# A state-space and feed-forward mix: the first strip moved ahead of tile 1's turns, and the second product cut at 384 columns instead of 512

## The chip, the cores and the metric

The kernel runs on one core of one Trainium2 chip. Times are device microseconds (us) of one execution of the program. A profile is one such execution, recorded instruction by instruction; its span, from the program's first instruction to its last, is about 1.8 us shorter than the time on the clock of the same run. A *run* below is one timed execution, and a *ratio* is the mean time of one kernel's fast runs over that of the other's of the same rounds, so it is not quite the ratio of the medians that are quoted.

Engines in the profile: PE is TensorE, PEld its weight loads, DVE is VectorE, ACT is ScalarE, POOL is GpSimd, SP issues most DMAs. "L268" is line 268 of that kernel. Lines shift by one to three between the two kernels.

## The reference

```python
x = A_x                                            # (1, 2048, 640) bf16
g = sigmoid((x * gate_w).sum(-1, keepdims=True))
# a: diagonal complex state space: Bu = x @ B_bar, h_t = Lam_bar * h_{t-1} + Bu_t, a = 2 Re(C h) + x * Dskip
# b: b = gelu(x @ w1 + b1) @ w2 + b2               # 640 -> 1728 -> 640
return g * a + (1 - g) * b
```

The sequence is taken in four chunks of 512 positions; a tile is 128 positions. Two parts matter here. The *first product* is x @ w1 for chunk 0, at the start of the program, while its data are still arriving. The *second product* is gelu(...) @ w2, once for each chunk.

## The kernel before

The start. TensorE needs x with the feature dimension on partitions. For chunk 0 it makes that itself: a *turn* is a product with the identity, whose result VectorE or ScalarE copies from PSUM to SBUF. A *strip* is six products of 128 columns, one for each of six PSUM banks: one tile's contribution of one block of 128 features. The warm-up products (ones times ones) use TensorE before any data is there.

```python
pA = bank()
for n in (512, 512, 512, 512, 512, 512, 128, 128):          # warm-up
    nc.tensor.matmul(pA[:, 0:n], lhsT=ones(P), rhs=ones(n), start=True, stop=True)
...
def turn_first(a, other):
    t = bank()
    turn(t, 0, a, 0)                                        # feature block 0 -> t, VectorE copies
    turned(nc.vector, t, 0, a, 0, 1)
    turn(other, a * P, a, 1)                                # feature block 1 -> other, ScalarE copies
    turned(nc.scalar, other, a * P, a, 1, 2)

turn_first(0, pA)
turn_first(1, bank())
...
banks = [bank() for _ in range(FA)]                         # FA = 6; the pool has 8 banks
...
part(0, 0)              # part(kd, a): the strip of feature block kd on tile a
part(0, 1)
turn_first(2, pA)
part(1, 0)
part(1, 1)
turn_first(3, pA)
part(0, 2)
turn_rest(0, bank(), (nc.scalar, KA, KD))                   # feature blocks 2 to 4 of tile 0
part(1, 2)
...
```

The second product. The 640 output columns of a tile are cut in a wide piece and a rest; each piece is 13 products (and one pair of half-row products). Two tiles' rests share a bank.

```python
MAIN, REST = (0, 512), (512, D)                             # D = 640
def biased(c, kind, i):                                     # ScalarE writes the bias into a fresh bank
    ...
    nc.scalar.activation(out=v, in_=src, func=ACT.Identity)
def fin_b(c, at={}):
    ...
    for h in range(2):
        for j in range(H):
            full(opened[c, "wide", a], 0, a, *MAIN)         # 13 products of 512 columns
            ...
        for j in range(H):
            full(opened[c, "rest", h], j * P, h * H + j, *REST)   # 13 products of 128 columns
        if h == 0:
            half_rows()
```

Of the kernel before, what the change touches and what calls it, by code (L numbers as in the profile page):

```python
# [16 lines left out]
P = 128  # L17
T = 2048
D = 640
# [9 lines left out]
H = TPC // 2  # L29
# [12 lines left out]
def kernel(  # L42
# [19 lines left out]
    nc = tc.nc  # L62
# [12 lines left out]
    def bank(dtype=F32):  # L75
        return ps.tile([P, CH * 4 // (4 if dtype == F32 else 2)], dtype, name="bank")
# [113 lines left out]
    class Clock:  # L190
        pe = 3.4
        act = 12.0
# [8 lines left out]
    def let_out(until, chunk=-1):  # L201
        while pend:
            ready, cost, fn, _ = pend[0]
            start = max(ck.dve, ready)
            if start >= until and not any(x[3] == chunk for x in pend if chunk >= 0):
                return
            pend.pop(0)
            fn()
            ck.dve = start + cost
# [6 lines left out]
    def pe(cols):  # L216
        ck.pe += cols / 2400.0 + 0.002

    def act(cost):
        ck.act = max(ck.act, ck.pe + 0.2) + cost  # L220
        return ck.act
# [4 lines left out]
    nc.vector.tensor_copy(out=tf[:], in_=tfi[:])  # L226
    ones = lambda n: nc.const_aps.tensor(1.0, [P, n], BF16)
    pA = bank()
    for n in (512, 512, 512, 512, 512, 512, 128, 128):
        nc.tensor.matmul(pA[:, 0:n], lhsT=ones(P), rhs=ones(n), start=True, stop=True)  # L230

    def turn(p, col, a, kd):
        nc.tensor.matmul(p[:, col:col + P], lhsT=xn[0][:, a, kd * P:(kd + 1) * P], rhs=ident[:], start=True, stop=True,  # L233
                         skip_group_check=True)

    def turned(engine, p, col, a, k0, k1):
        dst = xT[0][:, k0:k1, a * P:(a + 1) * P]
        src = p[:, col:col + (k1 - k0) * P].rearrange("p (k t) -> p k t", t=P)
        if engine is nc.vector:
            nc.vector.tensor_copy(out=dst, in_=src)  # L240
        else:
            nc.scalar.activation(out=dst, in_=src, func=ACT.Identity)  # L242

    def turn_first(a, other):
        t = bank()
        turn(t, 0, a, 0)
        turned(nc.vector, t, 0, a, 0, 1)
        turn(other, a * P, a, 1)
        turned(nc.scalar, other, a * P, a, 1, 2)

    turn_first(0, pA)
    turn_first(1, bank())

    def col(name, dtype=F32, n=KS):
        return const.tile([P, n], dtype, name=name)
# [68 lines left out]
    banks = [bank() for _ in range(FA)]  # L324

    def strip(kd, t0, t1, first, f0=0, f1=FA):
        for kf in range(f0, f1):
            ff1_mm(banks[kf], 0, kf, kd, t0, t1, first, 3)
# [30 lines left out]
    def part(kd, a):  # L359
        strip(kd, a * P, (a + 1) * P, kd == 0)  # L360

    part(0, 0)
    part(0, 1)
    turn_first(2, pA)
    part(1, 0)
    part(1, 1)
    turn_first(3, pA)
    part(0, 2)
# [217 lines left out]
            dve_now(ck.pe, 0.45, lambda: nc.vector.tensor_tensor(out=p[:, 0:d1 - d0], in0=xn[c][:, a, d0:d1], in1=Dbc[:, d0:d1], op=ALU.mult))  # L586
            seeded[ti].append(p)

    MAIN, REST = (0, 512), (512, D)
    opened = {}  # L590

    def biased(c, kind, i):
        p = bank()
        d0, d1 = MAIN if kind == "wide" else REST
        n = 1 if kind == "wide" else H
        v, src = p[:, 0:n * (d1 - d0)], b2bc[:, d0:d1]
        if n > 1:
            v = v.rearrange("p (j d) -> p j d", j=n)
            src = src.rearrange("p (o d) -> p o d", o=1).to_broadcast([P, n, d1 - d0])
        nc.scalar.activation(out=v, in_=src, func=ACT.Identity)  # L600
        act(0.6 if n == 1 else 0.4)
        opened[c, kind, i] = p

    def first_banks(c):
        biased(c, "wide", 0)
        biased(c, "wide", 1)

    def fin_b(c, at={}):
        def full(p, col, a, d0, d1):
            for kf in range(KF - 1):  # L610
                nc.tensor.matmul(p[:, col:col + d1 - d0], lhsT=gel[c][:, kf, a * P:(a + 1) * P], rhs=w2_sb[:, kf, d0:d1],  # L611
                                 start=False, stop=False, skip_group_check=True)
                pe(d1 - d0)

        def out_of(p, col, a, d0, d1):
            ti = c * TPC + a
            if gbs[ti] is None:
                gbs[ti] = fwork.tile([P, D], F32, name="gb")
            nc.scalar.activation(out=gbs[ti][:, d0:d1], in_=p[:, col:col + d1 - d0], func=ACT.Identity, scale=gcol[:, 1, ti:ti + 1])  # L619
            act(0.7 if d1 - d0 > 320 else 0.4)  # L620

        def half_rows():
            for d0, d1 in (MAIN, REST):
                for j in range(H):
                    for h in range(2):
                        p, col = (opened[c, "wide", h * H + j], 0) if d0 == 0 else (opened[c, "rest", h], j * P)
                        nc.tensor.matmul(p[:, col:col + d1 - d0], lhsT=gelL[c % 2][h * F_LAST:(h + 1) * F_LAST, j, :],  # L627
                                         rhs=w2l[h * F_LAST:(h + 1) * F_LAST, d0:d1], start=False, stop=True, skip_group_check=True)
                    pe(d1 - d0)
            ck.pe += 0.2  # L630

        biased(c, "rest", 0)
        biased(c, "wide", 2)
        for h in range(2):
            for j in range(H):
                a = h * H + j
                full(opened[c, "wide", a], 0, a, *MAIN)
                if a == 0:
                    biased(c, "wide", 3)
                    biased(c, "rest", 1)  # L640
                if h == 1:
                    out_of(opened[c, "wide", a], 0, a, *MAIN)
                if a in at:
                    at[a]()
                let_out(ck.pe)
            for j in range(H):
                full(opened[c, "rest", h], j * P, h * H + j, *REST)
            if h == 0:
                half_rows()
                for j in range(H):  # L650
                    out_of(opened[c, "wide", j], 0, j, *MAIN)
            for j in range(H):
                out_of(opened[c, "rest", h], j * P, h * H + j, *REST)
            let_out(ck.pe)

    def fin_a(c, at={}):
# [36 lines left out]
    ssm(1, {KS - 1: lambda: first_banks(0)})  # L693
    gates(1)
    fin_b(0, {a: (lambda a=a: fold(a)) for a in range(3)})
    gel_tile(2)
    ff1(2, 0, {1: lambda: fold(3), 4: lambda: fold(4), 9: lambda: seed(0), 11: lambda: seed(1)})
    gates(2)
    fin_a(0)
    load_xn(2)  # L700
    ssm(2, {KS - 1: lambda: first_banks(1)})
    fin_b(1, seeds(1))
    fin_a(1)
    load_xn(3)
    ssm(3)
    gel_tile(3)
    ff1(3, 0, {KF - 3: lambda: first_banks(2)})
    fin_b(2, seeds(2))
    gates(3)
    fin_a(2, {TPC - 1: lambda: first_banks(3)})  # L710
# [33 lines left out]
```

## Time and profile before

| | before |
|---|---|
| median, range of the 3 runs at hand | 216.24 us, 216.13 to 216.39 |
| profiled run: time, span | 215.6 us, 213.8 us |
| PE busy | 98% of the span |
| first product with the second block of w1's columns (w1b) starts | 12.45 us |
| last product starts | 210.87 us |

The profiled run is not one of the three timed ones, and it was 0.5 us shorter than the shortest of them.

The page's busy times and its chain of waits (the chain of work that ended last, as shares of the span):

```profile
PE 208.6 (98%) x1384; PEld 117.0 (55%) x1403; DVE 189.1 (88%) x389; ACT 103.4 (48%) x188; POOL 1.0 (0%) x13
...
PE 96%; DMA 1%; issue 1%; SPq 0%; DVE 0%; ACT 0%
```

TensorE is the chain almost throughout; the 1% of DMA is one load at the start. The timeline of PE shows it (columns: start, length of the group, engine, line, operation, form, how many, and in brackets the idle time before it and what ended that):

```profile
0.77 2.93 PE L230 MATMUL bank<-const-bfloat16-1.0 128*128 128x512 bf16 x8 [0.77 <-PEq L728]
3.50 0.42 PE L233 MATMUL bank<-ident,xn 128*128 128x128 bf16 x2
4.30 0.29 PE L233 MATMUL bank<-ident,xn 128*128 128x128 bf16 x2 [0.39 <-DMA xn<-in_A_x_dram]
4.42 1.08 PE L268 MATMUL bank<-xT,w1a 128*128 128x128 bf16 x12
5.34 0.28 PE L233 MATMUL bank<-ident,xn 128*128 128x128 bf16 x2
5.45 0.83 PE L268 MATMUL bank<-xT,w1a 128*128 128x128 bf16 x12
6.12 0.28 PE L233 MATMUL bank<-ident,xn 128*128 128x128 bf16 x2
6.23 0.50 PE L268 MATMUL bank<-xT,w1a 128*128 128x128 bf16 x6
6.72 0.33 PE L233 MATMUL bank<-ident,xn 128*128 128x128 bf16 x3
```

Read it in steps. The turns of tile 0 are the row at 3.50. Tile 1's turns wait until 4.30 for their load. The next twelve products take 1.08 us and the twelve after them 0.83: the first group stands still for 0.25 us after its fifth product, until a bank is free. Tile 3's turns (6.12) come after tile 2's (5.34); the turns at 6.72 come after tile 3's, and wait for tile 3's copy.

A group's length hides a second thing. The warm-up's products of 512 columns start 427 ns apart and those of 128 columns 107 ns apart; from 4.30 us on, 128 columns take 55.8 ns. The TensorE clock is halved at first. The trace's own clock record says "full" from 4.10 us on. The summary rows of granted clock do not show it: they give 1.0 from the start, because the record begins only with the first change.

### The profile page before, as it was taken

The page shows a single profiled execution, that of the slowest core. Times are in us where ns is not written, and L with a number is a line of the kernel's source. Part 1 is how long each engine was busy: PE and PEld are TensorE (multiplying, and loading weights), DVE is VectorE, ACT ScalarE, POOL GpSimd, SP SyncE. Part 2 cuts the span into 40 slices and gives each one's busy share as a digit, 9 for nine tenths or more (in the row PEclk, how much of TensorE's full clock was granted, in tenths as well). Part 3 has the DMA queues.
Part 4 walks back from the last instruction along what each step waited for, and adds up shares of the span by engine and source line. Part 5 has one row for each costly group of instructions (what it writes and reads, how often), then busy time and mean ns, then how long its engine had stood idle before and what let it go on. Part 6 is the DMA issues. An engine that isn't in the chain of part 4 may idle for free.

```text
span 213.8 us, 3572 instructions
## 1 busy us (share of the span) xinstructions
PE 208.6 (98%) x1384; PEld 117.0 (55%) x1403; DVE 189.1 (88%) x389; ACT 103.4 (48%) x188; POOL 1.0 (0%) x13
## 2 busy tenths in 40 slices
PE   7999999999999999999999999999999999999994
PEld 3845444454454544775445577444455577664773
DVE  1599999999999999999999999999999999983153
ACT  3699956675839688203563210455683422204200
POOL 1000000000000000000000000000000000000000
PEclk9999999999999999999999999999999999999999
DMA  6869999997000000051000006100000000100011
GB/s 192 243 157 191 205 186 290 313 210 185 0 0 0 3 0 0 14 183 65 0 0 3 0 0 186 62 0 2 3 0 14 0 3 31 61 34 0 0 66 61
DMA packets 31572, 15.84 MB, mean 74 GB/s; under 512 B 22979, under 2 KB 31555, under 8 KB 31555
## 3 DMA queue, kind: packets, MB, share of 16 engines
q1 hardware_dynamic: 30850, 14.99, 28.9%
q10 hardware_dynamic: 704, 0.62, 1.0%
q8 instruction: 11, 0.18, 0.4%
q14 instruction: 7, 0.05, 0.1%
HBM read 7.48 MB, written 2.62 MB: 47 GB/s over the span
## 4 chain that ended last, share of the span: by engine, by line
PE 96%; DMA 1%; issue 1%; SPq 0%; DVE 0%; ACT 0%
PE bank L611 26%; PE bank L268 26%; PE bank L670 20%; PE bank L553 20%; DMA xn<-in_A_x_dram 1%; PE bank L627 1%; PE bank L294 1%; PE bank L233 1%; SPq L136 0%; DVE ot L675 0%; ACT xT L242 0%; PE bank L284 0%; PE bank L402 0%; PE bank L371 0%
## 5 line engine op out<-in xcount | busy, mean ns | idle before, releaser
L611 PE MATMUL bank<-w_sb,gel 128*128 128x128 bf16 (+1 forms) x408 | 57.1, 298 | 0.6 <-issue 0.3
L611 PEld LDWEIGHTS <-gel 128*128 128x128 bf16 x416 | 32.2, 98 | 25.6
L556 ACT ACTIVATE bu<-bank 128x512 bf16<-128x512 f32 x40 | 23.7, 606 | 37.3 <-PE bank L553 37.3
L273 ACT ACTIVATE gel<-bank,colB 128x512 bf16<-128x512 f32 x52 | 33.7, 695 | 11.1 <-PE bank L268 10.4
L670 PEld LDWEIGHTS <-hs 128*128 128x128 bf16 x330 | 31.5, 98 | 11.6
L507 DVE TENSOR_TENSOR_SCAN g<-r_c,carry,v 128x512 bf16<-128x512 f32 x30 | 37.3, 1269 | 0.0
L619 ACT ACTIVATE gb<-bank,gcol 128x512 f32<-128x512 f32 (+1 forms) x32 | 15.1, 526 | 32.7 <-PE bank L627 17.8
L268 PE MATMUL bank<-xT,w1a 128*128 128x512 bf16 (+1 forms) x170 | 27.6, 311 | 0.3
L670 PE MATMUL bank<-CT_im,hs 128*128 128x320 bf16 (+2 forms) x165 | 27.1, 295 | 0.0
L670 PE MATMUL bank<-CT_re,hs 128*128 128x320 bf16 (+2 forms) x165 | 27.1, 295 | 0.0
L675 DVE SCALAR_TENSOR_TENSOR ot<-bank,gcol,gb 128x320 bf16<-128x320 f32 (+2 forms) x33 | 17.4, 532 | 8.9 <-PE bank L670 8.7
L553 PE MATMUL bank<-xT,BT_im 128*128 128x512 bf16 x99 | 24.8, 379 | 0.1
L553 PE MATMUL bank<-xT,BT_re 128*128 128x512 bf16 x97 | 24.5, 379 | 0.2
L268 PEld LDWEIGHTS <-w1a 128*128 128x128 bf16 x174 | 14.1, 98 | 11.7 <-issue 0.2
L268 PE MATMUL bank<-xT,w1b 128*128 128x512 bf16 x80 | 17.9, 379 | 0.0
L586 DVE TENSOR_TENSOR bank<-xn,Dbc 128x320 f32<-128x320 bf16 (+2 forms) x33 | 14.4, 480 | 3.7 <-ACT gb L619 3.6
L553 PEld LDWEIGHTS <-BT_im 128*128 128x128 bf16 x100 | 9.8, 98 | 11.8
L488 DVE TENSOR_TENSOR v<-wa,wb 128x512 bf16<-128x512 bf16 x40 | 15.2, 420 | 0.6
L553 PEld LDWEIGHTS <-BT_re 128*128 128x128 bf16 x100 | 9.6, 98 | 11.0
L600 ACT ACTIVATE bank<-b2bc 128x512 f32<-128x512 bf16 (+1 forms) x24 | 11.7, 526 | 6.7 <-DVE ot L675 6.7
L488 DVE TENSOR_TENSOR wa<-TCOS,g 128x1024 bf16<-128x1024 bf16 x20 | 13.7, 685 | 0.1
L268 PE MATMUL bank<-xT,w1c 128*128 128x512 bf16 x57 | 13.6, 379 | 0.2
(101 smaller groups left out, 166.4 us busy)
## 6 DMA issues: line engine op xcount, KB each, us to landing
out_dram<-ot SPq DMA_DIRECT2D x15, 160.0 KB, 1.8
w_sb<-in_B_w_dram SPq DMA_DIRECT2D x1, 2080.0 KB
xn<-in_A_x_dram SPq DMA_DIRECT2D x3, 640.0 KB
w1b<-in_B_w_dram SPq DMA_DIRECT2D x5, 128.0 KB, 3.7
w1c<-in_B_w_dram SPq DMA_DIRECT2D x5, 112.0 KB, 4.4
w1a<-in_B_w_dram ACTq DMA_DIRECT2D x2, 192.0 KB, 3.3
w1a<-in_B_w_dram SPq DMA_DIRECT2D x1, 384.0 KB, 3.7
xn<-in_A_x_dram SPq DMA_DIRECT2D x4, 64.0 KB, 3.3
```

The costliest lines, as they stand in the source:

```text
L268: nc.tensor.matmul(p[:, t0:t1], lhsT=w, rhs=xT[c][:, kd, t0:t1], start=(kd == 0) if first is None else first, stop=(kd == last), skip_grou ...
L273: nc.scalar.activation(out=gel[c][:, kf, :], in_=p[:, :], func=ACT.Gelu_apprx_tanh, bias=b1_c[:, kf:kf + 1])
L488: nc.vector.tensor_tensor(out=o, in0=a, in1=b, op=op)
L507: nc.vector.tensor_tensor_scan(s["g"][:, ri, :], r_c[:, ks:ks + 1].to_broadcast([P, CH]), s["v"][:, ri, :], init, ALU.mult, ALU.add)
L553: nc.tensor.matmul(p[:], lhsT=BT[ks >= KSA][:, kd, (ks % KSA if ks < KSA else ks - KSA) * P:][:, 0:P], rhs=xT[c][:, kd, :], start=(kd == 0 ...
L556: nc.scalar.activation(out=bu[:, ri, :], in_=p[:], func=ACT.Identity)
L586: dve_now(ck.pe, 0.45, lambda: nc.vector.tensor_tensor(out=p[:, 0:d1 - d0], in0=xn[c][:, a, d0:d1], in1=Dbc[:, d0:d1], op=ALU.mult))
L600: nc.scalar.activation(out=v, in_=src, func=ACT.Identity)
L611: nc.tensor.matmul(p[:, col:col + d1 - d0], lhsT=gel[c][:, kf, a * P:(a + 1) * P], rhs=w2_sb[:, kf, d0:d1], start=False, stop=False, skip_ ...
L619: nc.scalar.activation(out=gbs[ti][:, d0:d1], in_=p[:, col:col + d1 - d0], func=ACT.Identity, scale=gcol[:, 1, ti:ti + 1])
L670: nc.tensor.matmul(p[:, 0:d1 - d0], lhsT=hs[c][:, j, lo:lo + P], rhs=CT[:, j % KS, d0:d1], start=False, stop=(j == 2 * KS - 1), skip_group ...
L675: nc.vector.scalar_tensor_tensor(out=ot[:, d0:d1], in0=p[:, 0:d1 - d0], scalar=gcol[:, 0, ti:ti + 1], in1=gbs[ti][:, d0:d1], op0=ALU.mult, ...
```

## The change

Part A fills the wait for tile 1's load with the first strip, uses one bank fewer, shortens the warm-up, and puts three filler products under tile 0's copy. Part B cuts the second product at 384 columns, so that the pieces are more even (384 and 256 in place of 512 and 128).

```diff
-    for n in (512, 512, 512, 512, 512, 512, 128, 128):
+    for n in (512, 512, 512, 512, 512, 128, 128, 128, 128):
...
     turn_first(0, pA)
-    turn_first(1, bank())
...
+    for _ in range(3):
+        nc.tensor.matmul(banks[0][:, 0:P], lhsT=ones(P), rhs=ones(P), start=True, stop=True, skip_group_check=True)
     part(0, 0)
+    turn_first(1, pA)
+    part(1, 0)
     part(0, 1)
     turn_first(2, pA)
-    part(1, 0)
     part(1, 1)
     turn_first(3, pA)
...
-    MAIN, REST = (0, 512), (512, D)
+    WIDE = 3 * P
+    MAIN, REST = (0, WIDE), (WIDE, D)
```

The rest of the diff adapts column offsets (`j * P` to `j * (D - WIDE)`) and the cost figures by which the program, while it is built, orders VectorE's and ScalarE's work.

More of the change, by code (lines that the diff above doesn't have):

```diff
@@ L600, in biased @@
         nc.scalar.activation(out=v, in_=src, func=ACT.Identity)
-        act(0.6 if n == 1 else 0.4)
+        act(0.5 if n == 1 else 0.6)
         opened[c, kind, i] = p
@@ L619, in out_of @@
             nc.scalar.activation(out=gbs[ti][:, d0:d1], in_=p[:, col:col + d1 - d0], func=ACT.Identity, scale=gcol[:, 1, ti:ti + 1])
-            act(0.7 if d1 - d0 > 320 else 0.4)
+            act(0.56 if d1 - d0 > 320 else 0.45)
         def half_rows():
@@ L625, in half_rows @@
                     for h in range(2):
-                        p, col = (opened[c, "wide", h * H + j], 0) if d0 == 0 else (opened[c, "rest", h], j * P)
+                        p, col = (opened[c, "wide", h * H + j], 0) if d0 == 0 else (opened[c, "rest", h], j * (D - WIDE))
                         nc.tensor.matmul(p[:, col:col + d1 - d0], lhsT=gelL[c % 2][h * F_LAST:(h + 1) * F_LAST, j, :],
@@ L646, in fin_b @@
             for j in range(H):
-                full(opened[c, "rest", h], j * P, h * H + j, *REST)
+                full(opened[c, "rest", h], j * (D - WIDE), h * H + j, *REST)
             if h == 0:
@@ L652, in fin_b @@
             for j in range(H):
-                out_of(opened[c, "rest", h], j * P, h * H + j, *REST)
+                out_of(opened[c, "rest", h], j * (D - WIDE), h * H + j, *REST)
             let_out(ck.pe)
```

## The prediction

> **What bounds the kernel.** TensorE. The page gives PE 98% of the 213.8 us span, the chain of waits 96% on PE; the table of waits shows PE idle 1.5 us, nearly all before 4.3 us. DVE is 88% busy but PE does not wait for it after 7 us. Only PE time can move the result.
>
> **Part A, the start.** In the timeline of before: warm-up products from 0.77 us, one per 427 ns (512 columns) or 107 ns (128) at the low clock; turns of tile 0 at 3.50; idle until tile 1's load lands at 4.25; five strip products, then 0.25 us standing until ScalarE's copy (ends 4.90) frees a bank; then nearly gapless, 55.8 ns per 128-column product; tile 3's turns at 6.12.
> The change makes the warm-up 0.21 us shorter (first turn about 3.29), adds three fillers (0.3 us under the first copy, free), and puts strip 0 of tile 0 into the wait for tile 1's load. One bank fewer is taken, so the 0.25 us bank wait goes. Reckoned from those durations: strip 3.98 to 4.37, tile 1's turns, next strip 4.56 (second weight block lands 4.51), strip 0 of tile 1 at 4.98 (behind its copy), tile 2's turns 5.31, next strip until 5.76, where before stood at 6.12: 0.36 us ahead. But tile 3's load landed at 5.91, so its turns go at about 5.96 instead of 6.12: about 0.16 us survives. After it the order is as before, with the same copy waits, and later loads have slack.
>
> **Part B, 384 + 256 columns for 512 + 128.** Product and column counts stay (13 x 16 pairs plus half rows). Measured start to start: 215.5 ns at 512 columns, 55.8 at 128, 82.5 at 192: columns/2.4 plus about 2.4 ns, which agrees with the Trainium skill, "TensorE: Matmul & The Clock Gate", section "Back-to-back issue gap". A pair costs 271.3 ns before and, by that estimate, 271.5 after. The same section also states about 81 ns per product for a stream with weight loads at N=128; then the 128-column pieces would waste 25 ns x 208 = 5 us and this part would pay. The trace contradicts it: 26 in a row at 55.8 ns, each 98 ns weight load hidden. The switch into and out of the half rows costs 96 and 93 ns, by the drain, whatever the width. So part B is worth 0. ScalarE moves the same columns in as many instructions; VectorE's seeds come slightly earlier. Neither is on the chain.
>
> **Total.** 216.24 - 0.2 = **216.05 us**, range 215.7 to 216.35. Faster by over 2%: 0.01; within 2%: 0.98; slower by over 2%: 0.01.
>
> **What would show it.** A right: first strip near 4.0 us, no PE wait for tile 1's load, a short new wait for tile 3's load near 5.9, every later stage earlier by one constant 0.1 to 0.4 us. B right: stages of the second product last as long as before, PE idle unchanged, products spaced near 162 and 109 ns.
>
> **What would make it wrong.** The clock reached full at 4.10 us; if that comes later, strips run at 107 ns and the lead vanishes. If tile 3's load lands earlier, the gain nears 0.4 us. If narrow pieces cost something that the trace hides, B gains. If banks are freed later because 256-column pieces finish in pairs, PE waits at the next stage's start.

## More of the kernel before

ScalarE opens the banks with the bias and takes the results out.

In the last chunk, two such openings are placed just before the opening of the bank of the first product's last tile:

```python
ff1(3, 0, {KF - 3: lambda: first_banks(2)})     # first_banks: biased(c, "wide", 0), biased(c, "wide", 1)
# inside ff1, at the same step: last = last_bank(c)   (ScalarE opens it with b1x; TensorE waits for that)
```

## The result and the profile after

| | before | changed |
|---|---|---|
| median of 6 runs, range | 216.09 us, 215.83 to 216.39 | 215.68 us, 215.48 to 215.95 |
| ratio | | 0.998, 95% interval 0.9968 to 0.9993 |
| span of the profiled run | 213.8 us | 214.0 us |
| first w1b product | 12.45 us | 12.73 us |
| last product | 210.87 us | 211.06 us |
| clock record: full from | 4.10 us | 5.50 us |

The six runs of before include the three from which the prediction was made. The measured median lies 0.02 us below the predicted range. And the two profiles contradict the medians: the profiled run of the changed kernel is 0.2 us *longer* than that of before.

The page after, the same lines:

```profile
PE 210.5 (98%) x1407; PEld 126.5 (59%) x1407; DVE 189.4 (88%) x389; ACT 103.3 (48%) x188; POOL 1.0 (0%) x13
...
PE 98%; DVE 0%; issue 0%
```

The DMA share has left the chain, as intended. (The product counts are not comparable: by its weight loads the program has 1403 products before and 1407 after, one warm-up product and three fillers more, and 19 records are missing from the trace of before.) The timeline of PE after:

```profile
0.77 2.72 PE L230 MATMUL bank<-const-bfloat16-1.0 128*128 128x512 bf16 x9 [0.77 <-PEq L731]
3.29 0.42 PE L233 MATMUL bank<-ident,xn 128*128 128x128 bf16 x2
3.50 0.53 PE L362 MATMUL bank<-const-bfloat16-1.0 128*128 128x128 bf16 x3
3.98 0.80 PE L267 MATMUL bank<-xT,w1a 128*128 128x128 bf16 x6
4.57 0.42 PE L233 MATMUL bank<-ident,xn 128*128 128x128 bf16 x2
4.79 1.18 PE L267 MATMUL bank<-xT,w1a 128*128 128x128 bf16 x12
5.80 0.28 PE L233 MATMUL bank<-ident,xn 128*128 128x128 bf16 x2
5.91 0.50 PE L267 MATMUL bank<-xT,w1a 128*128 128x128 bf16 x6
6.40 0.27 PE L233 MATMUL bank<-ident,xn 128*128 128x128 bf16 x2
6.51 0.50 PE L267 MATMUL bank<-xT,w1a 128*128 128x128 bf16 x6
7.00 0.33 PE L233 MATMUL bank<-ident,xn 128*128 128x128 bf16 x3
```

The schedule does what was reckoned up to the strip at 3.98. Then six products take 0.60 us to the next row where the reckoning had 0.39, and the twelve at 4.79 take 1.01 us to the next row: TensorE still issues one per 107 ns up to 5.43 us, because in this run the clock became full only at 5.50 us. A second thing was not foreseen: tile 3's turns (6.40) now come only six products after tile 2's (5.80), and start 0.155 us later than these six at 55.8 ns each would allow. They wait for tile 2's copies to leave the banks; VectorE's ends at 6.35 us and ScalarE's at 6.39:

```profile
6.06 0.29 DVE L240 CAST xT<-bank 128x128 bf16<-128x128 f32 x1 [0.85 <-PE bank L233]
6.11 0.28 ACT L242 ACTIVATE xT<-bank 128x128 bf16<-128x128 f32 x1 [0.81 <-PE bank L233]
```

The same happens once more at 7.00. Before, only the later of these two waits existed.

Behind the start, the two traces can be compared almost without noise. These are the rows of the first w1b products, before and after, and the rows that end with the last product (five products 56 ns apart, of which the fifth is the program's last):

```profile
12.45 4.48 PE L268 MATMUL bank<-xT,w1b 128*128 128x512 bf16 x20
210.64 0.44 PE L670 MATMUL bank<-CT_im,hs 128*128 128x128 bf16 x5
12.73 4.48 PE L267 MATMUL bank<-xT,w1b 128*128 128x512 bf16 x20
210.84 0.44 PE L673 MATMUL bank<-CT_im,hs 128*128 128x128 bf16 x5
```

From the first w1b product to the last product, before takes 198.420 us (210.867 less 12.447) and the changed kernel 198.336 us; the stretch behind the last product takes 2.95 and 2.96 us. So all of the run-to-run scatter is in the first 12 us, and the change has gained 0.08 us behind the start, where the prediction had 0. The experiments below show that it is part B's (0.09 us there), and where.

### The profile page after: what moved, and what is told of

It is laid out like the page before. It is cut to its first block, busy times and chain, and to the rows that moved or that the text cites. A ratio compares the mean times of both kernels' runs of the same rounds, so it can differ in the third digit from the quotient of the medians.

```text
span 214.0 us, 3599 instructions
## 1 busy us (share of the span) xinstructions
PE 210.5 (98%) x1407; PEld 126.5 (59%) x1407; DVE 189.4 (88%) x389; ACT 103.3 (48%) x188; POOL 1.0 (0%) x13
## 4 chain that ended last, share of the span: by engine, by line
PE 98%; DVE 0%; issue 0%
PE bank L267 27%; PE bank L614 27%; PE bank L673 20%; PE bank L555 20%; PE bank L230 1%; PE bank L630 1%; PE bank L293 1%; PE bank L233 1%; DVE ot L678 0%; PE bank L362 0%; PE bank L283 0%; PE bank L404 0%; PE bank L373 0%
## 5 line engine op out<-in xcount | busy, mean ns | idle before, releaser
L614 PE MATMUL bank<-w_sb,gel 128*128 128x384 bf16 (+1 forms) x416 | 57.9, 300 | 0.0
L614 PEld LDWEIGHTS <-gel 128*128 128x128 bf16 x416 | 40.2, 98 | 17.1 <-issue 0.8
L272 ACT ACTIVATE gel<-bank,colB 128x512 bf16<-128x512 f32 x52 | 33.6, 695 | 10.5 <-PE bank L267 10.2
L622 ACT ACTIVATE gb<-bank,gcol 128x384 f32<-128x384 f32 (+1 forms) x32 | 15.1, 526 | 32.8 <-PE bank L614 16.6
L267 PE MATMUL bank<-xT,w1a 128*128 128x512 bf16 (+1 forms) x174 | 28.5, 319 | 0.0
L267 PEld LDWEIGHTS <-w1a 128*128 128x128 bf16 x174 | 14.9, 101 | 11.6
L603 ACT ACTIVATE bank<-b2bc 128x384 f32<-128x384 bf16 (+1 forms) x24 | 11.7, 526 | 7.6 <-DVE ot L678 7.6
```

The costliest lines, as they stand in the source:

```text
L267: nc.tensor.matmul(p[:, t0:t1], lhsT=w, rhs=xT[c][:, kd, t0:t1], start=(kd == 0) if first is None else first, stop=(kd == last), skip_grou ...
L272: nc.scalar.activation(out=gel[c][:, kf, :], in_=p[:, :], func=ACT.Gelu_apprx_tanh, bias=b1_c[:, kf:kf + 1])
L614: nc.tensor.matmul(p[:, col:col + d1 - d0], lhsT=gel[c][:, kf, a * P:(a + 1) * P], rhs=w2_sb[:, kf, d0:d1], start=False, stop=False, skip_ ...
L622: nc.scalar.activation(out=gbs[ti][:, d0:d1], in_=p[:, col:col + d1 - d0], func=ACT.Identity, scale=gcol[:, 1, ti:ti + 1])
```

## The experiments

Theory C: the moment at which the clock becomes full is not the kernel's but the run's; it moves the time by up to a microsecond, and a comparison of six runs with six runs carries its scatter. Theory D, which follows from it: the change itself is worth at most 0.1 us, and the rest of the 0.41 us was the draw. Rivals: the change really gains 0.4 us (more when the clock comes late); part B gives half of it.

### The kernels again, and each part alone

before_again and after_again are the two kernels unchanged. start_only is the changed kernel with the second product as before; pieces_only is the kernel before with

```diff
-    MAIN, REST = (0, 512), (512, D)
+    WIDE = 3 * P
+    MAIN, REST = (0, WIDE), (WIDE, D)
```

(and the offsets and cost figures that go with it).

Expected of before_again:

> The kernel before, unchanged, run under a second name: the noise of a comparison. All theories: ratio 1.000, within 0.1 us of the kernel before. Its profile gives a second sample of the moment at which the TensorE clock reaches full (4.10 us in the first profile). Theory C (the moment falls anywhere on a grid of 3.41 us, from run to run): a moment other than 4.10, and if later, first strips at 107 ns each and the whole span longer by up to half of the delay. Rival (the pattern of products sets the moment): 4.1 us again.

Expected of after_again:

> The changed kernel, unchanged. If the gain of 0.4 us is real: ratio 0.998, 0.3 to 0.5 us faster than the kernel before. If it was a lucky sample and the predicted 0.16 us is right: ratio 0.999. Theory C expects the clock's full moment elsewhere than 5.50 us; the rival expects 5.5 us again.

Expected of start_only:

> Part A alone (strip 0 ahead of tile 1's turns, shorter warm-up, fillers, one bank fewer); second product in 512 + 128 columns as before. Theory A (the whole gain lies in the start): the same ratio as the full change, 0.998, about 0.4 us faster. Rival B (the pieces give half of it): 0.999, about 0.2 us.

Expected of pieces_only:

> Part B alone (384 + 256 columns), start as before. Theory A: ratio 1.000, within 0.1 us of the kernel before. Rival B: about 0.2 us faster.

| run | median, range | ratio to before, 95% interval |
|---|---|---|
| before, 11 runs of the same rounds | 215.88 us, 215.20 to 216.38 | |
| before_again | 215.86 us, 215.43 to 216.43 | 1.0003, 0.9983 to 1.0023 |
| after_again | 215.93 us, 215.39 to 216.22 | 0.9999, 0.9979 to 1.0019 |
| start_only | 215.63 us, 215.33 to 216.34 | 0.9993, 0.9974 to 1.0012 |
| pieces_only | 215.93 us, 215.67 to 216.42 | 1.0006, 0.9988 to 1.0023 |

The gain did not come back: the changed kernel equals the kernel before. The scatter of one and the same kernel, over 1 us, is four times what the first three runs had shown (0.26 us). No single difference here is clear of it. The clock records gave full at 3.86 us (before_again) and 5.88 us (after_again): neither 4.10 nor 5.50 again, so the pattern of products does not set the moment.

What the times cannot tell, the traces can. The stretch from the first w1b product to the last takes 198.420 us in before_again and 198.425 in start_only, but 198.333 in pieces_only and 198.330 in after_again. So it is part B alone that takes 0.09 us out. The place is the last chunk's first product. ScalarE before, in the timeline:

```profile
157.32 1.11 ACT L600 ACTIVATE bank<-b2bc 128x512 f32<-128x512 bf16 x2
158.36 0.38 ACT L287 ACTIVATE bank<-b1x 128x260 f32<-128x260 bf16 x1
```

and in pieces_only:

```profile
157.48 0.90 ACT L601 ACTIVATE bank<-b2bc 128x384 f32<-128x384 bf16 x2
158.31 0.38 ACT L287 ACTIVATE bank<-b1x 128x260 f32<-128x260 bf16 x1
```

The PE rows that wait for that second ScalarE row, before:

```profile
155.89 2.97 PE L268 MATMUL bank<-xT,w1c 128*128 128x512 bf16 x13
158.79 0.77 PE L294 MATMUL bank<-w1c,xT 128*128 128x65 bf16 x20
```

and in pieces_only:

```profile
156.05 2.97 PE L268 MATMUL bank<-xT,w1c 128*128 128x512 bf16 x13
158.85 0.78 PE L294 MATMUL bank<-w1c,xT 128*128 128x65 bf16 x20
```

From the first to the second row of PE it is 2.90 us before and 2.80 with the new pieces. The L294 products accumulate onto what L287 wrote. ScalarE ends L287 at 158.74 before, after two bias openings of 512 columns; TensorE is ready for L294 at 158.70, 216 ns after the start of its last 512-column product at 158.48, and starts it 0.09 us after that, at 158.79. With openings of 384 columns ScalarE is done at 158.69 and TensorE, which gets to L294 at 158.85, does not wait.

The second product itself is as predicted. Its stage in chunk 1, from its first product to the first of the next stage, is 14.88 us in both (108.13 to 123.01 before, 108.41 to 123.29 after); 256-column products start 109 ns apart.

### With the clock full before the kernel begins

These kernels hold all loads and the original warm-up back for about 10 us behind a fixed chain of VectorE additions, and let TensorE run products meanwhile, so that the clock should be full before the kernel proper begins, at whatever moment of the run it becomes full. Only held kernels are compared with one another.

```diff
+    for _ in range(26):                                     # 36 in the held2 kernels
+        nc.tensor.matmul(pA[:, 0:512], lhsT=..., rhs=..., start=True, stop=True)
+    nc.vector.memset(hold[:], 0.0)
+    for _ in range(7):
+        nc.vector.tensor_tensor(out=hold[:], in0=hold[:], in1=hold[:], op=ALU.add)
+    nc.vector.tensor_copy(out=xn[0][:, 0, 0:1], in_=hold[:, 0:1])      # the first loads overwrite these
+    nc.vector.tensor_copy(out=w1a[0][:, 0:1], in_=hold[:, 0:1])
+    nc.vector.tensor_copy(out=pA[:, 0:1], in_=hold[:, 0:1])
     load_x0(nc.sync, 0, 1, 0, KA * P)
     load_w1a(nc.scalar, 0)
```

Expected of held_before:

> The kernel before, with everything held back some 9 us by a fixed chain of VectorE additions that the first loads wait for, while TensorE runs products, so that the clock is full before the kernel proper begins, whatever the phase. Takes about 9 us longer; only held kernels are compared with one another. Theory C (the moment of the full clock makes the spread of the runs, about 1 us): the six runs lie within 0.4 us of each other. Rival (something else, the loads say, makes the spread): still about 1 us.

Expected of held_after:

> The changed kernel, held back likewise. With the clock full from the start, the reckoning of the prediction applies (0.36 us of lead, of which tile 3's load lets 0.16 survive): 0.1 to 0.3 us faster than the held kernel before. If the measured 0.41 us is the change's own: 0.4 us faster.

Expected of held_start_only:

> Part A alone, held back. Theory A (all of the gain in the start): the same as the held change within 0.1 us.

Expected of held_pieces_only:

> Part B alone, held back. Theory A: the same as the held kernel before within 0.1 us. Rival B: 0.2 us faster.

| run | its runs, us | mean below 226.5 us |
|---|---|---|
| held_before | 227.27, 225.83, 225.83, 225.58, 227.31, 225.67 | 225.73 |
| held_after | 225.54, 225.50, 225.78, 225.62 | 225.61 |
| held_start_only | 225.40, 225.70, 225.46, 226.67, 225.66 | 225.56 |
| held_pieces_only | 227.36, 225.49, 226.13, 225.87, 227.27, 225.86 | 225.84 |

The hold worked in most runs and failed in an instructive way in five. The profile of held_before is one of those, its timeline of PE:

```profile
11.12 2.27 PE L242 MATMUL bank<-const-bfloat16-1.0 128*128 128x512 bf16 x8 [2.44 <-DVE bank L149]
13.18 0.42 PE L245 MATMUL bank<-ident,xn 128*128 128x128 bf16 x2
14.29 0.40 PE L245 MATMUL bank<-ident,xn 128*128 128x128 bf16 x2 [0.69 <-DMA xn<-in_A_x_dram]
14.48 1.49 PE L280 MATMUL bank<-xT,w1a 128*128 128x128 bf16 x12
```

TensorE had finished its 26 products and stood idle 2.44 us. The trace's clock record has full at 5.02 us, half at 11.85, full again at 18.68: the clock fell after the idle stretch, and the twelve products took 1.49 us. That run is 1.5 us longer than its neighbours (227.27 us against a mean of 225.73) with nothing else changed: on one kernel this shows that the clock alone can move the time by more than a microsecond. held_pieces_only's profile shows the same fall after an idle stretch of 2.26 us (half from 12.24 to 19.06 us); in the profiled runs of held_after and held_start_only a stretch of 1.72 and 1.73 us brought none. The three other runs above 226.5 us were not profiled, but each run has a mean granted clock: it is 0.985 in all five, which is what 6.8 us at half the clock make of 225 us, and 0.992 or 1.000 in the other sixteen. (The six with 0.992, by the same sum 3.4 us at half the clock, took 225.49 to 225.83 us and so lost nothing that can be seen.)

With 36 products there is no such idle stretch:

Expected of held2_before:

> The held kernel before with 36 products under the hold instead of 26, so that TensorE has no idle stretch of over 1.5 us in it and the clock cannot fall again. Theory C: no run at 227 us any more, all runs within 0.4 us.

Expected of held2_after:

> The changed kernel held in the same way. Theory: 0.1 to 0.2 us faster than held2_before (what the prediction reckoned for a full clock). If the change itself is worth the measured 0.41 us: 0.4 us.

Expected of held2_no_filler (the three filler products removed):

> The changed kernel held, without its three fillers. With the clock already full the fillers only occupy time under the first copy: equal to held2_after within 0.1 us. Rival (fillers cost, because the strip after them starts later): 0.1 us faster.

Expected of held2_bank_only (the kernel before with `turn_first(1, pA)` in place of `turn_first(1, bank())`):

> The kernel before, held, with one bank fewer taken for tile 1's turns and nothing else of the change: the 0.25 us stop at the fifth strip should go. If tile 3's load is what limits the start, 0.1 to 0.2 us faster than held2_before, as much as the whole change. If the reordering is what pays: under 0.05 us.

| run | runs | median, range | mean |
|---|---|---|---|
| held2_before | 5 | 225.59 us, 225.52 to 225.77 | 225.61 |
| held2_after | 4 | 225.63 us, 225.46 to 225.77 | 225.62 |
| held2_no_filler | 4 | 225.68 us, 225.33 to 226.02 | 225.68 |
| held2_bank_only | 4 | 225.78 us, 225.50 to 225.98 | 225.76 |

No run at 227 us any more, and every run of the held2 kernels has a mean granted clock of 0.999 or 1.000. With the clock out of the way the kernel before scatters by 0.25 us in five runs instead of over 1 us, as theory C expected; the two last kernels scatter by 0.69 and 0.48, more than the 0.4 expected, so the clock is the main source but not the only one. The landing of the loads is another: tile 1's load was issued at 11.43 us in held2_before and at 11.42 in held2_bank_only, and its turns, which wait for it in both, start at 14.49 and 14.24. Both held sets together (runs above 226.5 us left out) give 225.66 us for before (9 runs) and 225.62 for the changed kernel (8 runs): 0.05 us, with a standard error of 0.06. A gain of 0.4 us is excluded. Behind the start the traces have a gain of 0.09 us, which leaves -0.04 us for the start, with the same standard error: the predicted 0.16 at a full clock was too much. (The four runs of held_start_only alone are 0.1 us ahead of held2_before and held_before, with a standard error of 0.08.) The fillers and the bank by itself make no difference that these runs resolve; the fifth strip's wait gone alone is no gain.

Where the lead can go at a full clock, the timeline of PE in held_after shows (loads are issued from 10.96 us on, so subtract 10.2 to compare with the kernels that are not held):

```profile
14.22 0.29 PE L245 MATMUL bank<-ident,xn 128*128 128x128 bf16 x2
14.47 0.86 PE L279 MATMUL bank<-xT,w1a 128*128 128x128 bf16 x12
15.53 0.28 PE L245 MATMUL bank<-ident,xn 128*128 128x128 bf16 x2 [0.21 <-DMA xn<-in_A_x_dram]
15.65 0.50 PE L279 MATMUL bank<-xT,w1a 128*128 128x128 bf16 x6
16.14 0.27 PE L245 MATMUL bank<-ident,xn 128*128 128x128 bf16 x2
16.25 0.50 PE L279 MATMUL bank<-xT,w1a 128*128 128x128 bf16 x6
16.74 0.33 PE L245 MATMUL bank<-ident,xn 128*128 128x128 bf16 x3
```

Tile 2's turns, at 15.53, wait for tile 2's load (landed at 15.49): not tile 3's load, as predicted, but the one before it. After that each tile's turns come 0.61 us after the last ones although six strip products and two turns need 0.45 us (eight times 55.8 ns): the rest is the wait for the copy out of the only bank left for turns. In held2_before it takes 0.78 us from tile 2's turns to tile 3's (15.49 to 16.27) with twelve strip products between and no wait.

One profile is not the rule, though. In held2_after no turns after tile 0's wait for a load at first, and some of the lead goes later, to the load of feature blocks 2 to 4 of tiles 2 and 3:

```profile
18.12 0.34 PE L245 MATMUL bank<-ident,xn 128*128 128x128 bf16 x3 [0.15 <-DMA xn<-in_A_x_dram]
```

In held_start_only no load is waited for after tile 0's. The first w1b product comes at 22.47 us in held_after, 22.42 in held2_after and 22.25 in held_start_only, against 22.61 in held2_before, whose profiled run was the slowest of its five. So a load takes some of the lead in some runs, about 0.2 us by these figures, and nothing in others. In all three, tile 3's turns come 0.60 or 0.61 us after tile 2's, behind the copy and not behind tile 3's first load, which the prediction named.

### More runs of the kernels as they are, and a start with a late clock

after_b2 and after_b3 are the changed kernel, start_only_b2 is start_only again, no_warmup is the kernel before with

```diff
-    for n in (512, 512, 512, 512, 512, 512, 128, 128):
+    for n in (128,):
```

Expected of after_b2:

> The changed kernel again, not held, for the mean over many moments of the full clock. If the change is worth 0.41 us: six runs with a mean near 215.4, 0.4 us below the kernel before of the same rounds. Theory D (at most 0.1 us is the change's, the rest was the draw of six runs on each side): within 0.2 us of the kernel before of the same rounds, which has a mean of 215.8 again and not the 216.1 of the first comparison.

Expected of after_b3:

> The same kernel once more; the same expectations. The two together halve the error.

Expected of start_only_b2:

> Part A alone again, not held. Theory D: within 0.2 us of the kernel before of the same rounds. If part A is worth 0.4 us: 215.4.

Expected of no_warmup:

> The kernel before with one warm-up product of 128 columns in place of eight: TensorE is idle until 3.3 us, so the window in which it must be busy starts later. Theory C: full clock between about 5 and 8.5 us instead of about 2.5 to 6, and since each microsecond of it beyond 4.3 us costs 0.5 us, 0.7 to 1.2 us slower, with a spread of over 1 us. Rival (the moment of the full clock does not matter, loads and copies set the start): within 0.2 us of the kernel before.

| run | median, range | ratio to before, 95% interval |
|---|---|---|
| before, 11 runs of the same rounds | 215.95 us, 215.19 to 216.32 | |
| after_b2 | 216.01 us, 215.51 to 216.30 | 1.0010, 0.9991 to 1.0028 |
| after_b3 | 215.94 us, 215.66 to 216.25 | 1.0001, 0.9984 to 1.0019 |
| start_only_b2 | 215.56 us, 215.36 to 216.04 | 0.9989, 0.9972 to 1.0007 |
| no_warmup | 216.95 us, 216.04 to 217.68 | 1.0053, 1.0028 to 1.0077 |

The changed kernel is again not faster. Taking the products that only keep TensorE busy out of the warm-up costs 1.15 us (means of 217.01 and 215.86): the full clock came at 8.63 us in its profile, and the range widened to 1.64 us. So the moment of the full clock moves the time as theory C says. start_only is 0.14 and 0.21 us ahead of the kernel before of its rounds (12 runs, mean 215.67); the full change, which has the same start and by the traces a 0.09 us shorter remainder, is not (24 runs, mean 215.87). That is about twice the standard error of the difference (0.10), nearly three times when the 0.09 us is counted, and stays unexplained.

The last pair asked whether the change gains more when the clock is low through the whole start: no_warmup_b2 is no_warmup again, no_warmup_after is the changed kernel with the same one-product warm-up.

Expected of no_warmup_b2:

> The kernel before without its warm-up again, as the partner of the next run in the same rounds; theory: about 217.0 us, as in the first such run.

Expected of no_warmup_after:

> The changed kernel without its warm-up (fillers kept), so that its start always runs at the low clock. If the measured 0.41 us is what the change gains when the clock comes late: 0.4 us or more faster than no_warmup_b2. Theory D: the low clock makes TensorE's own 107 ns per product the limit, the waits that the change fills are short then, and it gains 0.1 to 0.3 us (0.09 of it not at the start but at 158 us), too little against a spread of over 1 us to be clear.

no_warmup_b2 took 217.08 us (216.82 to 217.71), no_warmup_after 216.79 us (216.12 to 217.22); the means differ by 0.42 us with a standard error of 0.25. That is inconclusive: it excludes neither 0.1 nor 0.4. In the two profiles (full from 7.54 and 7.17 us) tile 3's turns start at 7.09 and 6.78, so at a clock that is low all the time the reordering may well gain 0.3 us. In the real kernel the clock is never low that long.

### All profiles together

The profiles of kernels that were not held, as far as their trace has a clock record (those of start_only and pieces_only have none):

| profile | clock full from, us | first w1b product, us | from there to the last product, us |
|---|---|---|---|
| before_again | 3.86 | 12.27 | 198.420 |
| before | 4.10 | 12.45 | 198.420 |
| no_warmup_b2 (start of before) | 7.54 | 13.51 | 198.425 |
| no_warmup (start of before) | 8.63 | 13.90 | 198.419 |
| after_b2 | 3.62 | 12.44 | 198.333 |
| start_only_b2 | 5.44 | 12.72 | 198.425 |
| after | 5.50 | 12.73 | 198.336 |
| after_b3 | 5.75 | 12.85 | 198.332 |
| after_again | 5.88 | 13.11 | 198.330 |
| no_warmup_after (start of the change) | 7.17 | 13.21 | 198.330 |

The last column is fixed by the kind of pieces to within 0.01 us. The first two rise together. Between the first and the fourth row it is 0.34 us for each microsecond of delay (1.63 over 4.77), though the fourth kernel also lacks the warm-up; on that line the start of before would be at about 12.8 for a clock of 5.50 us and 13.0 for 5.88, an estimate, against 12.73 and 13.11 of the changed kernel. That is equality within the scatter of a few tenths that these rows show. With an early clock there is one profile of the changed kernel: in after_b2 (full from 3.62 us) tile 3's turns start at 6.03 us, near the predicted 5.96, but the first w1b product comes at 12.44, where before has 12.27 and 12.45.

## Why the prediction was wrong

**What bounds the kernel: right.** PE fills the chain, and everything behind 12.5 us repeats to 0.01 us.

**Part A's mechanism: right in kind, too large.** The strip did start near 4.0 us (3.98), the wait for tile 1's load and the stop at the fifth strip vanished, and a later load did take some of the lead in two of the held profiles. But "about 0.16 us survives. After it the order is as before, with the same copy waits" failed. With one bank left for turns of feature block 0 and six products between tile 2's and tile 3's turns, there is a second copy wait of 0.155 us that before did not have; and the load that bound at a full clock was not tile 3's first one but tile 2's in held_after and a later one in held2_after. Measured, at a full clock, both parts together: 0.05 us, standard error 0.06; less part B's 0.09, nothing is left for the start.

**Part B: right about the products, wrong by 0.09 us about the rest.** The stages are equal to 0.01 us and the pieces start 109 ns apart. The term that was not 0 was the ScalarE term ("Neither is on the chain"): two shorter bias openings let the last tile of the last chunk start without a wait of 0.09 us.

**The step that put the measured time outside the range was the total**: "216.24 - 0.2 = 216.05 us, range 215.7 to 216.35". Its base was the median of three runs that lie within 0.26 us; where its width of 0.65 us came from, it does not say. The profiled run of before, at 215.6 us, had already shown that the kernel does not keep within 0.26 us. In the 59 runs of the same kernel in later rounds the mean is 215.84 us, the standard deviation 0.34 and the range 215.19 to 216.56. The prediction named the clock's moment as something that could undo the lead; the runs showed it to be a scatter of every run, of both kernels. All 24 runs of the changed kernel together have a mean of 215.87 us, inside the predicted range: that the first six have a median outside it, by 0.02 us, is in good part a draw. The measured difference of 0.41 us did not return in any later comparison of the changed kernel: in the 18 further runs it has a mean of 215.93, 0.09 us above before, with a standard error of 0.08. With all runs, the first comparison included, the means are 215.86 us (before, 65 runs) and 215.87 (changed, 24 runs).

So the times put the change between a gain of about 0.17 and a loss of about 0.15 us (two standard errors about the 0.05 us of the held runs and about the -0.01 of all runs that were not held); 0.09 us of part B is what the traces show, and the start adds nothing that these runs resolve. In the first comparison before was 0.28 us above its later mean and the changed kernel 0.24 us below. When six and six are drawn at random from the pooled later runs, medians 0.41 us apart in this direction come up once in about 25 draws, means as far apart as there (0.43) once in about 90. What made the first comparison come out so is not settled, because its single runs have no profile but one each. Clock moments can do it. The chip is less likely: the five later jobs ran on four chips, and the kernel before had means of 215.78 to 215.90 us in them.

## What to carry to other kernels

Before predicting or measuring a change below half a percent, find out how much a run differs from the next and why; here the first 12 us carried all of it, so the time from a fixed instruction to the end told 0.09 us apart in two profiles where six against six timed runs could not tell 0.4. When a wait is filled by work from behind it, look at what that work used to hide: here strips that had covered a copy. And when ScalarE or VectorE is idle half of the time, still look for the one place where TensorE waits for its next result.

## What the Trainium skill lacked or had wrong

- "TensorE: Matmul & The Clock Gate", section "What's actually happening": it calls the window "free-running" and gives its length as 3413 ns. The traces agree: between full and the fall at the end of the program lie 61 or 62 windows of 3.413 us (213.709 less 5.496, over 61). But it gives the transition as varying by about 500 ns, though further down it reports 6, 11 or 14 slow products for one kernel; in the profiles of kernels whose first product is at 0.77 us with a warm-up of eight or nine products, full came between 3.62 and 5.88 us. Their first w1b products come between 12.27 and 13.11 us, beside a range of 1.4 us of all times.
- The same section advises not to fit a specific count of slow products, as the ramp is under 1% of a kernel. Here the whole spread of the kernel before is 0.6% (1.37 of 216 us), the clock is the main source of it, and it decides comparisons of tuned kernels. Holding the start back until the clock was full cut the scatter of this kernel to 0.25 us in five runs.
- The same page, the table of the section "Why this matters for your kernels", warns of idle gaps over about 3 us. In held_before an idle stretch of 2.44 us, with products on both sides of it in the same window, was enough: the clock fell at 11.85 us and the run was 1.5 us longer. In held_pieces_only 2.26 us were enough.
- The same page, section "Back-to-back issue gap", gives about 81 ns per product at 128 columns and 131 ns at 512 for streams with weight loads. The traces have 55.8 and 215.5 ns, which its formula for the isolated gap gives.
- No page that was used says that a summary of the granted clock can read 1.0 while products run at half rate: the record starts with the first change, and up to 4.10 us (before) products of 128 columns were 107 ns apart under a granted clock shown as 1.0.
